# One query token against 256 MB of cached keys and values: which engine sets how many parts of each key unit aside, and where the scratch lies

## The chip, the cores and the metric

The kernel runs on one core of one Trainium2 chip. The metric is the device time of one execution in microseconds (us), the median of several runs. Everything is float32.

## The reference

One token x of 512 elements goes through two branches, and a gate mixes them. Branch a is attention with 32 query heads over 8 key/value heads (four query heads share one) and 32,768 cached positions of 128 elements per key/value head. Branch b is a gated feed-forward block of width 1792.

```
g = sigmoid((x * gate_w).sum(-1))
q = x @ wq                                  # 512 -> 32 heads x 128
scores = q . k_cache * 128 ** -0.5          # 8 kv heads x 32768 positions
o = softmax(scores) . v_cache
a = o @ wo                                  # 4096 -> 512
b = (silu(x @ w1) * (x @ w3)) @ w2          # 512 -> 1792 -> 512
out = g * a + (1 - g) * b
```

k_cache and v_cache have 134 MB each, the weights together some 28 MB. Each byte is used once for one token, so 296 MB must come from HBM.

## The kernel before

**Units.** The keys are cut into 16 units of 8 MB, the values too. Unit t of the keys holds a quarter of the positions of two key/value heads: 128 partitions with 64 KB each, the first 32 KB from the one head (z = 0), the second from the other (z = 1). There are two big buffers, `big_a` and `big_b`, of a unit each (R = 8192 elements is half a unit in one partition). By `where` (L301) key units 0 and 2 go to big_b, all the others to big_a; wq starts in big_a. From the fifth unit on, big_b holds value units.

**A key unit.** Keys lie with the position along the partitions and must be turned. A half unit (z) is cut into four parts c of 32 of the head's 128 elements; a part has 64 x 32 = 2048 elements in each partition. For each part DVE transposes 32 x 32 blocks into `kt0` or `kt1` in turn (L336), and PE multiplies the result with the window of queries, four products (L323). So a unit takes eight transposes, (z, c) from (0, 0) to (1, 3). Of these, the last two, (1, 2) and (1, 3), don't read the big buffer: when the unit has landed, ScalarE copies them into `wo_t` (L311 to L313, `set_aside`), a tile of 16 KB in a partition that will hold a quarter of wo at the end of the kernel. So the big buffer is free after six transposes and ScalarE's copy.

**Order and waits.** The program is written out by `Program.add` (L44), which works out from the keys that each operation reads and writes on which semaphores it waits. Key "A0" is the first half of big_a, "A1" the second, "wo" the tile wo_t. The writing of a buffer waits for its readers. A transpose of keys carries a credit instead of a count (`credit="keys"`, L336): PE takes it in a hardware loop (L679, L684), and whoever must wait for the transpose waits for the PE product that took it (L65 to L66, `via`). PE's instructions inside the loops wait on credits alone (`take`, L665).

**The loop over units** (L465 to L489), for key unit t and, four units behind (LAG = 4), value unit v = t - 4: `set_aside(t)`; the eight parts, with ScalarE's copy of the query window before each half (L317); ScalarE takes the scores out of PSUM (L342); SP issues key unit t + 1 into its buffer; DVE sums up value unit v - 1 (`own`); after every fourth unit the scores are turned by PE (L352) and normalised by DVE and ScalarE (`softmax`, L360 to L389); PE multiplies the value unit v from big_b with its weights (L413); SP issues value unit v + 1 into big_b. After the fourth key unit (t = 3) w1 and w3 are loaded into big_b ahead of key unit 4, multiplied (`hidden_products`, L437), and `hidden` (L452) forms the feed-forward's inner vector on ScalarE and DVE, with row0 as scratch.

**The end** (L576 on): value units 12 to 15 through both big buffers, between them the four quarters of wo into wo_t, which DVE multiplies in (`mix`, L539), and last w2 in five pieces into big_a.

**Queues.** All large loads are issued by SP, one after the other, so an issue that waits holds up those behind it. x, gate_w and the output go by ScalarE's queue. x and gate_w land in `row0` and `row1` (L173, L199), which then hold the queries for a moment (L283 to L286).

Of the kernel before, what the change touches and what calls it, by code (L numbers as in the profile page):

```python
# [116 lines left out]
def kernel(  # L117
# [13 lines left out]
    nc = tc.nc  # L131
    _, HKV, S, DH = k_cache.shape
    D = x.shape[-1]
    F = w1.shape[1]
    HQ = wq.shape[1] // DH
    REP = HQ // HKV
    NC = D // P
# [6 lines left out]
    NB = 64  # L144
    R = NB * DH
    NP = HKV // 2
    NH = 4 * NP
    LAG = 4
    FR = F // P
    FJ = F // 4  # L150
# [4 lines left out]
    pr = Program(nc, tc.alloc_semaphore)  # L155
    pe, dve, act, pool = (
        lambda fn, _e=e, **kw: pr.add(_e, fn, **kw) for e in ("PE", "DVE", "ACT", "POOL")
    )
    V, A, T = nc.vector, nc.scalar, nc.tensor

    def sbuf(name, *shape):
        return nc.alloc_sbuf_tensor(name, [P, *shape], F32)[:]

    big = [sbuf("big_a", 2 * R), sbuf("big_b", 2 * R)]
    wo_t = sbuf("wo_t", 8, D)
    kt = [sbuf(f"kt{i}", NB * 32) for i in range(2)]
    sb = sbuf("sb", 16, 32, 4)
    win = sbuf("win", NP, 4, 48)
# [1 line left out]
    probs = sbuf("probs", 2, 65 * 16)  # L170
    prob = [probs[:, u, :] for u in range(2)]
    pv = sbuf("pv", 33 * 16)
    rows = [sbuf(f"row{i}", 512) for i in range(2)]  # L173
    tmp = sbuf("tmp", 2, 4, P)
    silu = tmp[:, 0].rearrange("p b d -> p (b d)")
    red = [sbuf(f"red{h}", P) for h in range(6)]
    acc = sbuf("acc", 512)
    otp = sbuf("otp", 8, 32)
    htp = sbuf("htp", FR, 32)
# [7 lines left out]
    def load(dst, src, writes, over=()):  # L187
        lanes[0] += 1
        lane = f"load{lanes[0] % 12}"
        return pr.add(  # L190
            "SP", lambda: nc.sync.dma_start(dst, src), writes=writes, over=[*over, lane], inc=lane, by=16, also=lane,  # L191
        )

    def region(b, z):
        return big[b][:, z * R:(z + 1) * R]
# [11 lines left out]
    mt, mtt, mark = sbuf("mt", 32), sbuf("mtt", 32), sbuf("mark", 1)  # L207
# [14 lines left out]
    for src, dst, view, axes in (  # L222
# [9 lines left out]
        s = tiles[src][:, 0:16] if src == "fold" else tiles[src]  # L232
        dve(lambda s=s, d=tiles[dst], v=view, a=axes: V.tensor_reduce(d, s.rearrange(v, **a), axis=AX.X, op=ALU.add),
            reads=[src], writes=[dst])
# [24 lines left out]
    for c in range(NC):  # L259
# [19 lines left out]
        reads=["gate0"], writes=["gate1"])  # L279
# [4 lines left out]
    for b in range(2):  # L284
        qt = kt[b][:, 0:512]
        dve(lambda b=b, qt=qt: V.transpose(qt, rows[b]), reads=[f"row{b}"], writes=[f"kt{b}"])  # L286
        for j in range(4):
            w, u = divmod(4 * b + j, 2)
            src = qt[32 * j:32 * j + 32, :].rearrange("p (q c x) -> p x c q", q=4, c=4)[:, 0]
            for e in range(2):  # L290
                r, o = 2 * u + e, 16 + 8 * e + 4 * u
                dst = win[32 * r:32 * r + 32, w, :, o:o + 4]
# [6 lines left out]
    vd = v_cache.rearrange("a h (e p n) d -> (a h) e p (n d)", e=2, p=P)  # L299

    def where(t):  # L301
        return 1 if t in (0, 2) else 0
# [3 lines left out]
        load(big[b], kd[t // 4, t % 4], ["AB"[b] + str(z) for z in range(2)])  # L306


    spare = wo_t.rearrange("p k e -> p (k e)").rearrange("p (n r) -> p n r", n=NB)

    def set_aside(t):  # L311
        src = region(where(t), 1).rearrange("p (n r) -> p n r", n=NB)[:, :, 64:128]
        act(lambda: A.copy(spare, src), reads=["AB"[where(t)] + "1"], writes=["wo"])  # L313

    def window(t, z):
        return act(
# [4 lines left out]
    def scores_part(c):  # L321
        for g in range(4):
            ins = T.matmul(  # L323
                ps_s[32 * g:32 * g + 32, :], winc[:, c, :], kt[c % 2][:, 512 * g:512 * g + 512],
                start=False, stop=False, skip_group_check=True,
            )
        return ins

    def scores(t, z, win_op):
        kin = region(where(t), z).rearrange("p (n c j) -> p c n j", c=4, j=32)  # L330
        for c in range(4):
            src, key = kin[:, c], "AB"[where(t)] + str(z)
            if (z, c) >= (1, 2):
                src, key = spare[:, :, 32 * (c - 2):32 * (c - 2) + 32], "wo"
            dst = kt[c % 2].rearrange("p (n i) -> p n i", i=32)
            k = dve(lambda d=dst, s=src: V.transpose(d, s), reads=[key], writes=[f"kt{c % 2}"], credit="keys")  # L336
            pe(lambda c=c: scores_part(c), reads=[f"kt{c % 2}", "winc"], writes=["s"], loop=True,
               credits=((win_op, 1), (k, 1)) if c == 0 else ((k, 1),))
# [20 lines left out]
    def softmax(w):  # L359
        banks = [f"f{f}" for f in range(4)]  # L360

        dve(lambda: V.tensor_reduce(mt[:, 0:8], turned.rearrange("p (n q) -> p q n", q=8), axis=AX.X, op=ALU.max),  # L362
            reads=banks, writes=["mt"])
        dve(lambda: V.transpose(mtt, mt), reads=["mt"], writes=["mtt"])
        for k in range(4):
            dve(lambda k=k: V.tensor_reduce(quads[0:32, k:k + 1], mtt[32 * k:32 * k + 32, :], axis=AX.X, op=ALU.max),  # L366
                reads=["mtt"], writes=[("quads", k)])
        dve(lambda: V.tensor_reduce(high[0:32, :], quads[0:32, :], axis=AX.X, op=ALU.max),
            reads=[("quads", k) for k in range(4)], writes=["high"])
        for k in range(4):  # L370
            dve(lambda k=k: V.tensor_copy(wide_t[32 * k:32 * k + 32, :], high[0:32, :].to_broadcast([32, 32])),
                reads=["high"], writes=[("wide_t", k)])
        dve(lambda: V.transpose(top, wide_t), reads=[("wide_t", k) for k in range(4)], writes=["top"])
        dve(lambda: V.tensor_tensor(  # L374
            turned.rearrange("p (n q) -> p n q", q=8), turned.rearrange("p (n q) -> p n q", q=8),
            top[:, 0:8].unsqueeze(1).to_broadcast([P, 256, 8]), op=ALU.subtract,
        ), reads=["top"], writes=banks)

        act(lambda: A.copy(mark, ones[:, 0:1]), reads=["ones"], writes=["mark"])
        for u in range(2):  # L380
            act(lambda u=u: A.activation(  # L381
                prob[u][:, 0:1024].rearrange("p (y n q) -> p n y q", y=16, q=4),
                turned.rearrange("p (n y u q) -> p n y u q", n=16, y=16, u=2)[:, :, :, u],
                AF.Exp, scale=SCALE,
            ), reads=[*banks, "mark"], writes=[("prob", u)])
        dve(lambda: V.tensor_reduce(  # L386
            sums[:, 8 * w:8 * w + 8].rearrange("p (u q) -> p u q", u=2),
            probs[:, :, 0:1024].rearrange("p u (n q) -> p u q n", q=4), axis=AX.X, op=ALU.add,
        ), reads=[("prob", u) for u in range(2)], writes=[("sums", w)])  # L389


    def load_values(s):
        return load_credit(big[1], vd[s // 2, s % 2], ["B0", "B1"])

    def load_credit(dst, src, writes):
        return pr.add("SP", lambda: nc.sync.dma_start(dst, src), writes=writes, credit="values", by=16)

    def weights(s):
        u, e = s // 2 % 2, s % 2
# [32 lines left out]

    def load_hidden():
        for z, t in enumerate((w1, w3)):
            load(region(1, z)[:, 0:NC * F], t.rearrange("(p c) f -> p (c f)", c=NC), [f"B{z}"])

    def hidden_products():  # L437
        for z in range(2):
            def ff(z=z):
                t = region(1, z)  # L440
                for c in range(NC):
                    for j in range(4):
                        o = c * F + FJ * j
                        ins = T.matmul(
                            pm[z][32 * j:32 * j + 32, 0:FJ], xp[:, c, :], t[:, o:o + FJ],
                            start=(c == 0), stop=(c == NC - 1),
                        )
                return ins
            pe(ff, reads=[f"B{z}", "xp"], writes=[f"m{z}"])


    def hidden():  # L452
        act(lambda: A.activation(silu[:, 0:FJ], pm[0][:, 0:FJ], AF.Sigmoid), reads=["m0"], writes=["tmp0"])
        dve(lambda: V.tensor_mul(silu[:, 0:FJ], silu[:, 0:FJ], pm[0][:, 0:FJ]), reads=["m0", "tmp0"], writes=["tmp0"])
        dve(lambda: V.scalar_tensor_tensor(
            rows[0][:, 0:FJ].rearrange("p (k a) -> p k a", k=FR), silu[:, 0:FJ].rearrange("p (a k) -> p k a", k=FR),
            gate[:, 1:2], pm[1][:, 0:FJ].rearrange("p (a k) -> p k a", k=FR), op0=ALU.mult, op1=ALU.mult,
        ), reads=["tmp0", "gate1", "m1"], writes=["row0"])
        dve(lambda: V.transpose(htp.rearrange("p k a -> p (k a)"), rows[0][:, 0:FJ]), reads=["row0"], writes=["htp"])


    load_keys(0)
# [184 lines left out]
    for a, b in parts[2:]:  # L647
        ff_down([(htp[:, k, :], w2t[:, k, :], k == 8, k == FR - 1) for k in range(a, b)], reads=["htp", ("w2", a)])
        if a == 8:
# [4 lines left out]
           reads=["res"], inc="row", by=16)  # L654
# [6 lines left out]
    a, b, c, d = flips  # L661
# [63 lines left out]
```

## Time and profile before

| what | value |
|---|---|
| runs | 702.02, 701.26, 701.96 us; median 701.96 |
| the profiled execution, its own time | 699.78 us |
| its span, first to last instruction | 697.7 us |
| mean granted TensorE clock | 0.795 |
| PE, DVE, ScalarE busy | 374.9, 374.6, 105.5 us |
| read from HBM | 296.23 MB, 425 GB/s over the span |
| transposes of keys (L336) | 128, of 2274 to 2285 ns |
| copies aside (L313) | 16, of 3606 to 3607 ns |

The page gives the busy time of each engine, the span in 40 slices, the DMA queues, the chain of work that ended last, and the costliest groups of instructions by line, each with the idle time of its engine ahead of it and what ended that wait. The timeline gives the start and length of each instruction, SP's issues of transfers among them; the trace has also the start and length of each DMA packet. A packet here is what one partition gets from one transfer, so a unit is 128 packets of 64 KB over 16 DMA engines.

### The profile page before, as it was taken

The numbers are of one execution on the slowest core, as the hardware profiler recorded it, in microseconds if no ns is written. First come the engines' busy times: TensorE is split into PE (matmuls) and PEld (weight loads), VectorE is DVE, ScalarE is ACT, GpSimd is POOL, SyncE is SP. The second block draws the span as 40 slices with busy tenths as digits, with TensorE's granted clock in tenths as the row PEclk, the third lists the DMA queues.
The fourth block names the chain that finished last, engine by engine and source line by source line (L and its number), as shares of the span: only waits on it lengthen the run. The fifth ranks groups of instructions, "written<-read, shape, count | busy, mean of one in ns | idle before, by whom it ended". The sixth has DMA issues, their size and how long they took to land. (4 is left out here: it accounts for less than half of the span.)

```text
span 697.7 us, 5701 instructions
## 1 busy us (share of the span) xinstructions
PE 374.9 (54%) x2400; PEld 87.9 (13%) x2400; DVE 374.6 (54%) x263; ACT 105.5 (15%) x112; POOL 2.6 (0%) x15
## 2 busy tenths in 40 slices
PE   1536555555473736466463636474573726565376
PEld 0100100201010101101010101101010101221012
DVE  1049988591734628591725536790816436744121
ACT  0132221320202121120202121210202021100000
POOL 1000000000000000000000000000000000000000
PEclk9958999879687878978696877778687966777589
DMA  9999999999999999999999999999999999999996
GB/s 410 429 421 421 417 412 419 430 428 425 421 447 436 425 428 428 440 432 428 436 428 421 440 443 429 428 425 436 436 440 432 417 432 421 428 452 429 417 417 287
DMA packets 6644, 296.34 MB, mean 425 GB/s; under 512 B 742, under 2 KB 746, under 8 KB 1132
## 3 DMA queue, kind: packets, MB, share of 16 engines
q1 hardware_dynamic: 6624, 296.23, 98.9%
q8 instruction: 5, 0.08, 0.0%
q14 instruction: 3, 0.02, 0.0%
q10 hardware_dynamic: 12, 0.01, 0.0%
HBM read 296.23 MB, written 0.00 MB: 425 GB/s over the span
## 5 line engine op out<-in xcount | busy, mean ns | idle before, releaser
L323 PE MATMUL ps<-kt,winc 128*32 128x512 f32 x1024 | 182.7, 792 | 238.7 <-PEq L667 238.7
L336 DVE STREAM_TRANSPOSE kt<-big_a 128x2048 f32<-128x2048 f32 x84 | 187.1, 2285 | 182.0 <-DMA big_a<-in_A_k_cache_dram 182.0
L413 PE MATMUL ps<-big_b,pv 128*32 128x512 f32 x768 | 89.3, 619 | 0.0
L313 ACT COPY wo_t<-big_a 128x4096 f32<-128x4096 f32 x14 | 50.5, 3606 | 174.0 <-DMA big_a<-in_A_k_cache_dram 174.0
L323 PEld LDWEIGHTS ps<-kt,winc 128*32 128x32 f32 x1024 | 26.3, 121 | 391.0 <-issue 391.0
L336 DVE STREAM_TRANSPOSE kt<-wo_t 128x2048 f32<-128x2048 f32 x32 | 71.6, 2274 | 0.0
L239 PE MATMUL ps<-acc 128*128 128x512 f32 x34 | 26.3, 866 | 21.8 <-PEq L667 20.3
L342 ACT COPY sb<-ps 128x512 f32<-128x512 f32 x16 | 17.1, 1067 | 135.1 <-PE ps L323 135.1
L541 DVE SCALAR_TENSOR_TENSOR acc<-wo_t,own_rows,acc 128x512 f32<-128x512 f32 x24 | 18.0, 752 | 32.1 <-DMA wo_t<-in_A_wo_dram 31.3
L336 DVE STREAM_TRANSPOSE kt<-big_b 128x2048 f32<-128x2048 f32 x12 | 26.7, 2284 | 11.1 <-DMA big_b<-in_A_k_cache_dram 11.1
L413 PEld LDWEIGHTS ps<-big_b,pv 128*32 128x32 f32 x768 | 23.8, 114 | 65.6 <-issue 65.6
L317 ACT COPY winc<-win 128x128 f32<-128x128 f32 x32 | 9.8, 307 | 109.8 <-PE ps L323 109.7
L554 PE MATMUL ps<-big_b,probs 128*32 128x512 f32 x128 | 18.0, 718 | 13.9 <-DMA big_b<-in_A_v_cache_dram 13.9
L554 PE MATMUL ps<-big_a,probs 128*32 128x512 f32 x128 | 18.5, 742 | 11.3 <-DMA big_a<-in_A_v_cache_dram 11.3
L362 DVE TENSOR_REDUCE mt<-turned 128x8 f32<-128x2048 f32 x4 | 9.2, 2292 | 24.0 <-PE turned L352 24.0
L386 DVE TENSOR_REDUCE sums<-probs 128x8 f32<-128x2048 f32 x4 | 14.9, 3737 | 10.8 <-ACT probs L381 10.8
L265 PE MATMUL turned<-big_a,xp 128*32 128x512 f32 x64 | 9.0, 725 | 11.9 <-DMA big_a<-in_A_wq_dram 11.9
L429 DVE TENSOR_REDUCE red<-tmp 128x128 f32<-128x1024 f32 x6 | 11.6, 1926 | 0.2
L239 PEld LDWEIGHTS ps<-acc 128*128 128x128 f32 x34 | 6.3, 232 | 39.3 <-issue 37.7
L381 ACT ACTIVATE probs<-turned 128x1024 f32<-128x1024 f32 x8 | 7.8, 1021 | 22.4 <-DVE turned L374 22.3
L278 DVE TENSOR_SCALAR gate<-gate 128x1 f32<-128x1 f32 x1 | 0.2, 155 | 20.0 <-ACT gate L277 20.0
L352 PEld LDWEIGHTS turned<-ident,sb 128*128 128x128 f32 x64 | 9.3, 169 | 3.3 <-issue 3.3
(85 smaller groups left out, 123.2 us busy)
## 6 DMA issues: line engine op xcount, KB each, us to landing
wo_t<-in_A_wo_dram SPq DMA_DIRECT2D x4, 2048.0 KB, 18.1
big_b<-in_B_w_dram SPq DMA_DIRECT2D x2, 3584.0 KB, 19.9
big_b<-in_A_v_cache_dram SPq DMA_DIRECT2D x1, 4096.0 KB, 27.4
big_b<-in_A_v_cache_dram SPq DMA_DIRECT2D x2, 2048.0 KB, 34.0
big_a<-in_B_w_dram SPq DMA_DIRECT2D x2, 1024.0 KB, 21.2
big_a<-in_B_w_dram SPq DMA_DIRECT2D x1, 768.0 KB, 23.7
big_a<-in_B_w_dram SPq DMA_DIRECT2D x1, 512.0 KB, 24.4
big_a<-in_B_w_dram SPq DMA_DIRECT2D x1, 256.0 KB, 24.6
```

What stands on the lines that cost most here:

```text
L239: return T.matmul(ps_s, acc[:, 0:P], acc, start=True, stop=False, skip_group_check=True)
L313: act(lambda: A.copy(spare, src), reads=["AB"[where(t)] + "1"], writes=["wo"])
L317: lambda: A.copy(winc, win[:, t // 4, :, 16 - 16 * z:48 - 16 * z]),
L323: ins = T.matmul(ps_s[32 * g:32 * g + 32, :], winc[:, c, :], kt[c % 2][:, 512 * g:512 * g + 512], start=False, stop=False, skip_group_chec ...
L336: k = dve(lambda d=dst, s=src: V.transpose(d, s), reads=[key], writes=[f"kt{c % 2}"], credit="keys")
L342: lambda: A.copy(sb[:, :, :, t % 4], ps_s.rearrange("p (n i) -> p n i", i=32)),
L352: ins = T.transpose(pf[f][:, P * a:P * a + P], sb[:, 4 * f + a].rearrange("p i m -> p (i m)"), ident)
L386: dve(lambda: V.tensor_reduce(sums[:, 8 * w:8 * w + 8].rearrange("p (u q) -> p u q", u=2), probs[:, :, 0:1024].rearrange("p u (n q) -> p u ...
L413: ins = T.matmul(ps_o[32 * t:32 * t + 32, :], pv[:, o:o + 32], big[1][:, n * P:(n + 4) * P], start=((z, g) == (0, 0)), stop=((z, g) == (1, ...
L429: dve(lambda: V.tensor_reduce(red[h], tmp.rearrange("p e b d -> p d (e b)"), axis=AX.X, op=ALU.add), reads=["tmp0", "tmp1"], writes=[("red ...
L541: dve(lambda k=k: V.scalar_tensor_tensor(acc, wo_t[:, k, :], own_rows[:, w, k:k + 1], acc, op0=ALU.mult, op1=ALU.add,), reads=["wo", ("own ...
L554: ins = T.matmul(ps_o[32 * t:32 * t + 32, :], prob[u][:, o:o + 32], vt[:, n * P:(n + 4) * P], start=((e, z, g) == (0, 0, 0)), stop=((e, z, ...
```

## The change

ScalarE sets three parts of each key unit aside in place of two: (1, 1), (1, 2) and (1, 3). The tile for them, `aside`, has 24 KB in a partition; wo_t becomes its first 16 KB. Of key unit 3 (t = LAG - 1) a fourth part, (1, 0), is copied as well, by a second copy, into the last 8 KB of big_b, which is free at that time. So that it stays free, w3 is loaded right behind w1 (from element 7168 of big_b in place of 8192) and the two end at element 14336. The first value unit overwrites that place and waits for the part's reader too (`over=["extra"]`).

The tiles row0 and row1 go: x, gate_w and the queries use the first 1024 elements of `probs` half 0, where the softmax puts its weights later, and the softmax's Exp waits for the readers of row0 and row1. `hidden` uses the second half of `tmp` in place of row0.

```diff
-    wo_t = sbuf("wo_t", 8, D)
+    aside = sbuf("aside", NB * 96)
+    wo_t = aside[:, 0:8 * D].rearrange("p (k e) -> p k e", k=8)
...
-    rows = [sbuf(f"row{i}", 512) for i in range(2)]
+    rows = [probs[:, 0, 512 * i:512 * i + 512] for i in range(2)]
     tmp = sbuf("tmp", 2, 4, P)
-    silu = tmp[:, 0].rearrange("p b d -> p (b d)")
+    silu, prod = (tmp[:, i].rearrange("p b d -> p (b d)") for i in range(2))
...
-    spare = wo_t.rearrange("p k e -> p (k e)").rearrange("p (n r) -> p n r", n=NB)
+    spare = aside.rearrange("p (n r) -> p n r", n=NB)
+    extra = big[1][:, 2 * NC * F:2 * R].rearrange("p (n r) -> p n r", n=NB)

     def set_aside(t):
-        src = region(where(t), 1).rearrange("p (n r) -> p n r", n=NB)[:, :, 64:128]
-        act(lambda: A.copy(spare, src), reads=["AB"[where(t)] + "1"], writes=["wo"])
+        src, key = region(where(t), 1).rearrange("p (n r) -> p n r", n=NB), "AB"[where(t)] + "1"
+        act(lambda: A.copy(spare, src[:, :, 32:128]), reads=[key], writes=["wo"])
+        if t == LAG - 1:
+            act(lambda: A.copy(extra, src[:, :, 0:32]), reads=[key], writes=["extra"], over=["B1"])
...
-            if (z, c) >= (1, 2):
-                src, key = spare[:, :, 32 * (c - 2):32 * (c - 2) + 32], "wo"
+            if (z, c) >= (1, 1):
+                src, key = spare[:, :, 32 * (c - 1):32 * (c - 1) + 32], "wo"
+            elif z == 1 and t == LAG - 1:
+                src, key = extra, "extra"
...
-            ), reads=[*banks, "mark"], writes=[("prob", u)])
+            ), reads=[*banks, "mark"], writes=[("prob", u)], over=["row0", "row1"])
...
-        return load_credit(big[1], vd[s // 2, s % 2], ["B0", "B1"])
-
-    def load_credit(dst, src, writes):
-        return pr.add("SP", lambda: nc.sync.dma_start(dst, src), writes=writes, credit="values", by=16)
+        return pr.add(
+            "SP", lambda: nc.sync.dma_start(big[1], vd[s // 2, s % 2]), writes=["B0", "B1"], over=["extra"],
+            credit="values", by=16,
+        )
...
-            load(region(1, z)[:, 0:NC * F], t.rearrange("(p c) f -> p (c f)", c=NC), [f"B{z}"])
+            load(big[1][:, z * NC * F:(z + 1) * NC * F], t.rearrange("(p c) f -> p (c f)", c=NC), [f"B{z}"])
...
-                t = region(1, z)
+                t = big[1][:, z * NC * F:(z + 1) * NC * F]
...
-            rows[0][:, 0:FJ].rearrange("p (k a) -> p k a", k=FR), silu[:, 0:FJ].rearrange("p (a k) -> p k a", k=FR),
+            prod[:, 0:FJ].rearrange("p (k a) -> p k a", k=FR), silu[:, 0:FJ].rearrange("p (a k) -> p k a", k=FR),
             gate[:, 1:2], pm[1][:, 0:FJ].rearrange("p (a k) -> p k a", k=FR), op0=ALU.mult, op1=ALU.mult,
-        ), reads=["tmp0", "gate1", "m1"], writes=["row0"])
-        dve(lambda: V.transpose(htp.rearrange("p k a -> p (k a)"), rows[0][:, 0:FJ]), reads=["row0"], writes=["htp"])
+        ), reads=["tmp0", "gate1", "m1"], writes=["tmp1"])
+        dve(lambda: V.transpose(htp.rearrange("p k a -> p (k a)"), prod[:, 0:FJ]), reads=["tmp1"], writes=["htp"])
```

## The prediction

> **What bounds the kernel now.** The page's second part first, then its third.
>
> ```profile
> DMA  9999999999999999999999999999999999999996
> GB/s 410 429 421 421 417 412 419 430 428 425 421 447 436 425 428 428 440 432 428 436 428 421 440 443 429 428 425 436 436 440 432 417 432 421 428 452 429 417 417 287
> q1 hardware_dynamic: 6624, 296.23, 98.9%
> ```
>
> DVE and PE are busy 54% of the span, the 16 DMA engines 98.9% of it, all by SP's one queue. So nothing that an engine does matters unless it delays a transfer, and I looked for the time that the queue loses. Next, the groups by shape:
>
> ```profile
> L336 DVE STREAM_TRANSPOSE kt<-big_a 128x2048 f32<-128x2048 f32 x84 | 187.1, 2285 | 182.0 <-DMA big_a<-in_A_k_cache_dram 182.0
> L313 ACT COPY wo_t<-big_a 128x4096 f32<-128x4096 f32 x14 | 50.5, 3606 | 174.0 <-DMA big_a<-in_A_k_cache_dram 174.0
> L317 ACT COPY winc<-win 128x128 f32<-128x128 f32 x32 | 9.8, 307 | 109.8 <-PE ps L323 109.7
> L401 ACT COPY pv<-probs 128x512 f32<-128x512 f32 x12 | 7.5, 621 | 0.0
> ```
>
> Then the landings of the key units: where ScalarE's copy (L313) or DVE's first transpose begins out of a wait for the DMA (the timelines of both):
>
> ```profile
> 102.30 13.28 DVE L336 STREAM_TRANSPOSE kt<-big_a 128x2048 f32<-128x2048 f32 x6 [2.25 <-DMA big_a<-in_A_k_cache_dram]
> 140.54 3.61 ACT L313 COPY wo_t<-big_a 128x4096 f32<-128x4096 f32 x1 [3.05 <-DMA big_a<-in_A_k_cache_dram]
> 179.40 3.61 ACT L313 COPY wo_t<-big_a 128x4096 f32<-128x4096 f32 x1 [17.22 <-DMA big_a<-in_A_k_cache_dram]
> 218.22 3.61 ACT L313 COPY wo_t<-big_a 128x4096 f32<-128x4096 f32 x1 [17.43 <-DMA big_a<-in_A_k_cache_dram]
> 257.66 3.61 ACT L313 COPY wo_t<-big_a 128x4096 f32<-128x4096 f32 x1 [18.67 <-DMA big_a<-in_A_k_cache_dram]
> 296.36 3.61 ACT L313 COPY wo_t<-big_a 128x4096 f32<-128x4096 f32 x1 [5.37 <-DMA big_a<-in_A_k_cache_dram]
> ```
>
> I call the key units K0 to K15, the value units V0 to V15. One key and one value unit lie between most landings, and the quickest such pair takes 38.69 us (K12 at 451.58 to K13 at 490.27). A unit alone takes 19.35 (K0 43.66 to K1 63.01). The trace's record of each DMA packet agrees: a 64 KB packet takes 2.418 us on one engine, each engine has 8 in a unit, 8 x 2.418 = 19.34. w1 and w3 take 16 packets of 1.062 = 16.99. Against that floor the landings lose: K2 0.04, K3 0.57, K4 1.91 (140.54 - 102.30 = 38.24 against 16.99 + 19.34), K5 0.17, K6 0.13, K7 0.75, K9 0.06, K12 0.37, K15 1.05, the others 0.02 or less: 5.13 us from K0 to K15 (568.72). From K15 to wo's third part (660.93) come four units and three parts of wo, 77.38 + 14.69 = 92.07 us by packets, and 92.21 pass: 0.12 or so more. After that the queue is full to the end. In all 5.25 us are lost.
>
> Where, is told by SP's timeline beside the packets:
>
> ```profile
> 78.37 0.33 SPq L191 DMA_DIRECT2D big_a<-in_A_k_cache_dram  x1
> 117.71 0.33 SPq L191 DMA_DIRECT2D big_a<-in_A_k_cache_dram  x1
> 131.56 0.33 SPq L396 DMA_DIRECT2D big_b<-in_A_v_cache_dram  x1
> 156.12 0.33 SPq L191 DMA_DIRECT2D big_a<-in_A_k_cache_dram  x1
> 233.70 0.33 SPq L191 DMA_DIRECT2D big_a<-in_A_k_cache_dram  x1
> ```
>
> A key unit is issued only shortly before the first DMA engine has finished the transfer ahead of it. I call the time between the two the lead: K3 1.98 us (80.35 - 78.37), K4 -0.29 (117.42 - 117.71), K5 1.84, K7 2.17, K12 2.20, K15 2.00, V12 1.97 (it follows K15 into big_a); K2, K6, K8 to K11, K13 and K14 2.4 to 3.1. Value units have 5.9 to 9. Averaged over the 16 engines, waiting and overlong first packets cost 0.1 to 0.9 us where the lead is under 2.5 (1.7 at K4), 0.03 to 0.19 between 2.6 and 3.1, about 0.03 with a value unit. By landings: leads under 2.3 lose 0.12 to 1.91, those of 2.4 to 3.1 lose 0.04 on average, long ones none.
>
> What holds the issue:
>
> ```profile
> SPq L191 <- PE ps L323: 191.4, 18, 14.5
> SPq L110 <- ACT wo_t L313: 178.9, 15, 15.0
> ```
>
> SP waits for ScalarE's copy first and for PE last: a transpose tells SP nothing itself, the scores product (L323) that takes it does. K5: six transposes out of big_a from 141.55, 13.30 us, the product 1.27 later, issue at 156.12.
>
> **The change, part by part.**
> Three parts set aside: five transposes read the unit where six did, so SP is released one transpose earlier, 13.3 / 6 = 2.22 us (2.28 by the group's row). Every lead of K2 to V12 grows by that. The unit is transposed eight times as before, and a transpose from the set-aside tile costs 2274 ns against 2285.
> ScalarE's copy: three rows of copies (128 elements 307 ns, 512 in 621, 4096 in 3606) lie on 0.19 + 0.833 per 1000 elements, so 6144 take 5.31 us, 1.70 more, 16 times. It begins at the landing; the first transpose that reads it is now the sixth, 11.1 us after the landing, and the release comes at 11.1 + 1.3. The cover is 5.8 us. The window copy queued behind it on ScalarE waits for PE's fourth product anyway, about 10 us after the landing. Cost nothing; without that cover it would be 1.7 a unit.
> The fourth unit (K3): another copy of 2048 elements, 1.90 us. Both end 7.2 us after ScalarE starts at 102.38; four transposes and a product end at 102.30 + 8.9 + 1.3 or later. K4's lead grows by two transposes, to 4.2. The new waits (big_b's tail free, V0 after its reader) look back at products finished some 9 us before the copy, and at a transpose finished before K4's landing, while V0 waits for w1's and w3's products as now.
> The scratch: x and gate_w land in a probs half that nothing else uses before 132; the softmax's added wait is for readers done by 35 us. w3 lies right behind w1, same bytes. hidden() writes tmp where it wrote row0, same shapes. Nothing, each bounded by the 0.65 to 0.98 us of such a row, once, on DVE around 140 (below, K5).
>
> **What is late next.** Leads of 4.2 to 5.3 do not occur in the trace. They lie between those of 2.4 to 3.1 (0.04 lost on a landing) and those above 5.9 (0.01): I take 0.03, the ends being 0.01 and 0.13 (K6). K5 is different: DVE works off the softmax and hidden() until 141.64 and only then begins K4. K4 will land 2.5 us earlier (0.04 + 0.57 + 1.91), at 138.0, but DVE comes free only as much earlier as K3 lands, 0.61, at 141.0. K5 goes out at 141.0 + 11.1 + 1.3 = 153.4, and the engines want it at 157.96 - 2.52 = 155.4: a lead of 2.0. There I leave the mean of the landings with leads of 1.8 to 2.2 (0.57, 0.17, 0.75, 0.37, 1.05, 0.12): 0.5, ends 0.1 and 1.05.
> Sum: 5.25 - 0.5 - 14 x 0.03 = **4.3 us** saved, and the last DMA and what follows it (1.5 us from 693.45) move with it. The profiled execution took 699.78 for a span of 697.7; it would be 695.5. The runs shown have 701.96, 2.2 above it, with the same kernel; I take the difference as staying: 697.7.
>
> **A rule that speaks against most of this.** The first packet of K4 begins 1.20 us after its issue (117.71 to 118.91), that of wq 1.23, and K4's last engine starts at 120.42, 2.71 after. The Trainium skill, "DMA: Bandwidth & Descriptors", Specifications, gives about 0.6 us to the first byte for a DMA issued from SP. By it a lead of 1.8 would do and only K4 pay; the trace speaks for a longer time, with overlong packets at leads up to 2.5.
>
> **Rivals.**
> Only the dry queue counts: a lead above the 1.2 us to the first packet is enough, and what K3, K7, K12 and K15 lose is a drift between engines that comes whatever the lead. Then K4's 1.91 goes, or, of it, the 1.24 in which its engines stood empty: 700.1 to 700.7. For it: K9 had overlong packets (0.53 on average) and lost only 0.06 on its landing. Against it: no value unit shows such a loss. 0.13.
> Nothing that can be measured: the early engines' stalls shrink, but the slowest engine of each transfer sets its landing and keeps its pace, so under 0.7 us goes: 701.5. 0.06.
> It doesn't do what it says: SP is still released by the sixth product. Then K4 alone gains little; the same 701.5, and counted with the case before.
> Slower: ScalarE's copy becomes the last to release big_a. It decides from a copy longer than the 14.6 us that the release takes now, and three quarters of a unit would have to cost 4 times the row of half a unit. At 16 us the leads shrink by 1.4, to about 1, and 15 key transfers lose what lies between K15's 1.05 and K4's 1.91, less what they lose now: some 1.2 x 15 = 18 us, 720. Nothing in the rows speaks for it, and the transposes beside the copy are no slower than the others (2285 against 2274 ns). 0.04.
>
> **How the numbers follow.** Forecast 0.77, rivals as above. 697.7 is the likeliest. The low end: the 5.25 whole and 0.4 of spread between runs (701.26 to 702.02), 696.3. The high end takes in the dry-queue case, 700.7. A measurement can tell some 0.2%, 1.4 us, from no change. Faster: the forecast and half of the dry queue, 0.84; within: the other half and the third case, 0.12; slower 0.04.
>
> **What would show it.** ScalarE's copy at 5.3 us in SP's wait, ended by a PE product 12.4 us after the landing; K4 issued near 112.5 with DMA work still queued; the pairs of landings at 38.69 to 38.75 save K4 to K5; no packet group overlong at a key unit's start. Wrong it would be if pairs still lost 0.4 to 1 with leads above 4, if the transposes slowed beside the longer copy, or if a loss moved to the value units.

## The result and the profile after

The changed kernel takes 697.22 us in the median of 9 runs (695.61 to 698.32), the kernel before 701.72 in 9 runs beside it (698.87 to 702.72): a ratio of 0.9936, interval 0.9921 to 0.9951, 4.5 us. The forecast was 697.7 against 701.96, a gain of 4.3. The profiled execution took 695.61 us with a span of 693.5, against 699.78 and 697.7: 4.2 us, where the sum was 4.3.

The page after, first the DMA queue, then the groups of the transposes and of the copies aside:

```profile
q1 hardware_dynamic: 6624, 296.23, 99.1%
L343 DVE STREAM_TRANSPOSE kt<-big_a 128x2048 f32<-128x2048 f32 x69 | 154.1, 2288 | 179.2 <-DMA big_a<-in_A_k_cache_dram 178.3
L316 ACT COPY aside<-big_a 128x6144 f32<-128x6144 f32 x14 | 74.4, 5313 | 169.5 <-DMA big_a<-in_A_k_cache_dram 169.5
L343 DVE STREAM_TRANSPOSE kt<-aside 128x2048 f32<-128x2048 f32 x48 | 106.6, 2271 | 0.0
```

DVE makes as many transposes (69 and 48 in these rows, 11 more out of big_b), no slower; the copy is the 5.31 us of the prediction. ScalarE is busy 134.6 us in place of 105.5, and that shows nowhere in the time. SP's timeline after has the issues of K4, V0, K5, K6 and K7:

```profile
111.91 0.33 SPq L192 DMA_DIRECT2D big_a<-in_A_k_cache_dram  x1
130.95 0.33 SPq L401 DMA_DIRECT2D big_b<-in_A_v_cache_dram  x1
153.34 0.33 SPq L192 DMA_DIRECT2D big_a<-in_A_k_cache_dram  x1
190.24 0.33 SPq L192 DMA_DIRECT2D big_a<-in_A_k_cache_dram  x1
228.70 0.33 SPq L192 DMA_DIRECT2D big_a<-in_A_k_cache_dram  x1
```

K4 is issued 5.8 us earlier than before (117.71), 4.3 us before the first DMA engine has finished w3 (116.18 by the packets). Times of packets are given here as the trace has them, on the same axis as SP's issues. The prediction's stand 0.23 us later: it has the first packet of K4 at 118.91, and the trace has it at 118.68. So all its leads are 0.23 us too long (K3 1.75, K4 -0.52, K5 1.62, K7 1.94, K12 1.97, K15 1.77); their order and its sum don't change by it.

ScalarE's timeline after has the landings of K4 to K8:

```profile
138.22 5.31 ACT L316 COPY aside<-big_a 128x6144 f32<-128x6144 f32 x1 [1.33 <-DMA big_a<-in_A_k_cache_dram]
177.59 5.31 ACT L316 COPY aside<-big_a 128x6144 f32<-128x6144 f32 x1 [15.06 <-DMA big_a<-in_A_k_cache_dram]
216.29 5.31 ACT L316 COPY aside<-big_a 128x6144 f32<-128x6144 f32 x1 [17.97 <-DMA big_a<-in_A_k_cache_dram]
255.00 5.31 ACT L316 COPY aside<-big_a 128x6144 f32<-128x6144 f32 x1 [18.01 <-DMA big_a<-in_A_k_cache_dram]
293.69 5.32 ACT L316 COPY aside<-big_a 128x6144 f32<-128x6144 f32 x1 [5.37 <-DMA big_a<-in_A_k_cache_dram]
```

From 177.59 on the pairs are 38.69 to 38.71 us apart, the floor; K7, which lost 0.75 before, loses nothing, and K15, which lost 1.05, 0.02. K3 lands at 101.76 (before 102.30), K4 36.46 behind it (38.24). The one pair that still loses is K4 to K5, 39.37: 0.68. DVE's timeline shows why:

```profile
135.06 3.75 DVE L393 TENSOR_REDUCE sums<-probs 128x8 f32<-128x2048 f32 x1 [3.34 <-ACT probs L388]
138.73 0.61 DVE L461 TENSOR_TENSOR tmp<-tmp,ps 128x448 f32<-128x448 f32 x1
139.38 0.99 DVE L462 SCALAR_TENSOR_TENSOR tmp<-tmp,gate,ps 128x448 f32<-128x448 f32 x1
140.40 0.65 DVE L466 STREAM_TRANSPOSE htp<-tmp 128x448 f32<-128x448 f32 x1
140.97 11.10 DVE L343 STREAM_TRANSPOSE kt<-big_a 128x2048 f32<-128x2048 f32 x5
```

K4 has landed by 138.22, and DVE is still at the softmax and hidden() until 140.97. So K5 goes out at 153.34 with a lead of 1.53.

### The profile page after: what moved, and what is told of

Same layout as the page of the kernel before. It is cut to its first block, busy times and chain, and to the rows that moved or that the text cites. A ratio compares the mean times of both kernels' runs of the same rounds, so it can differ in the third digit from the quotient of the medians.

```text
span 693.5 us, 5702 instructions
## 1 busy us (share of the span) xinstructions
PE 367.7 (53%) x2400; PEld 86.7 (13%) x2400; DVE 374.4 (54%) x263; ACT 134.6 (19%) x113; POOL 2.6 (0%) x15
## 5 line engine op out<-in xcount | busy, mean ns | idle before, releaser
L328 PE MATMUL ps<-kt,winc 128*32 128x512 f32 x1024 | 177.6, 772 | 238.5 <-PEq L674 238.5
L343 DVE STREAM_TRANSPOSE kt<-big_a 128x2048 f32<-128x2048 f32 x69 | 154.1, 2288 | 179.2 <-DMA big_a<-in_A_k_cache_dram 178.3
L316 ACT COPY aside<-big_a 128x6144 f32<-128x6144 f32 x14 | 74.4, 5313 | 169.5 <-DMA big_a<-in_A_k_cache_dram 169.5
L343 DVE STREAM_TRANSPOSE kt<-aside 128x2048 f32<-128x2048 f32 x48 | 106.6, 2271 | 0.0
L548 DVE SCALAR_TENSOR_TENSOR acc<-aside,own_rows,acc 128x512 f32<-128x512 f32 x24 | 18.0, 752 | 34.6 <-DMA aside<-in_A_wo_dram 33.8
L240 PE MATMUL ps<-acc 128*128 128x512 f32 x34 | 24.1, 799 | 21.8 <-PEq L674 20.3
L343 DVE STREAM_TRANSPOSE kt<-big_b 128x2048 f32<-128x2048 f32 x11 | 24.5, 2282 | 9.6 <-DMA big_b<-in_A_k_cache_dram 9.6
L316 ACT COPY aside<-big_b 128x6144 f32<-128x6144 f32 x2 | 10.6, 5312 | 5.4 <-DMA big_b<-in_A_k_cache_dram 5.4
```

Of the source, the lines that this page charges most:

```text
L240: return T.matmul(ps_s, acc[:, 0:P], acc, start=True, stop=False, skip_group_check=True)
L316: act(lambda: A.copy(spare, src[:, :, 32:128]), reads=[key], writes=["wo"])
L328: ins = T.matmul(ps_s[32 * g:32 * g + 32, :], winc[:, c, :], kt[c % 2][:, 512 * g:512 * g + 512], start=False, stop=False, skip_group_chec ...
L548: dve(lambda k=k: V.scalar_tensor_tensor(acc, wo_t[:, k, :], own_rows[:, w, k:k + 1], acc, op0=ALU.mult, op1=ALU.add,), reads=["wo", ("own ...
```

## The experiments

My theory: what a key unit loses depends on its lead, and the longer leads are the whole gain. The rivals: only the dry queue at K4 counted, or something else in the change brought the gain. The times below are medians; a ratio is to runs of the kernel before on the same chip, whose medians were 701.1 to 701.3.

**The longer lead of K4 alone** (e1): two parts aside for each unit, four for K3.

```diff
+        lo = 1 if t == LAG - 1 else 2
-        act(lambda: A.copy(spare, src[:, :, 32:128]), ...)
+        act(lambda: A.copy(spare[:, :, 32 * (lo - 1):96], src[:, :, 32 * lo:128]), ...)
...
-            if (z, c) >= (1, 1):
+            if (z, c) >= (1, 1 if t == LAG - 1 else 2):
```

> The changed kernel, but with two parts set aside for every key unit except K3, which keeps its four. Only K4 has the longer lead. My theory (every key unit's lead counts): K2, K3 and K6 to V12 lose again what they lost before, about 3 us on the landings, K4 nothing, and K5, which now has neither the old late landing of K4 nor the earlier release, has a lead near 0.4 us and loses 1 to 1.5: in all some 4 us above the changed kernel, 701, about 0.8 under the kernel before. The rival (only a queue that runs dry costs, so K4 was all of the gain): within 1 us of the changed kernel, 697 to 698.

701.06 us, ratio 0.9988 (0.9966 to 1.001). The time is the one expected, but the trace gets there another way. K3 loses 1.8, and from K3 (103.48) to K5 (181.71) pass 78.23 us against a floor of 75.03: K4's gain comes back as a loss of 3.2 at K5, where I had expected 1 to 1.5. K6 to K15, which were to lose again what they lost before, lose 0.5 in all, 0.4 of it at K12. SP's timeline of this kernel, K4, V0, K5:

```profile
113.70 0.33 SPq L192 DMA_DIRECT2D big_a<-in_A_k_cache_dram  x1
134.19 0.33 SPq L402 DMA_DIRECT2D big_b<-in_A_v_cache_dram  x1
159.69 0.33 SPq L192 DMA_DIRECT2D big_a<-in_A_k_cache_dram  x1
```

K5 is issued 3.6 us after the first engine has come free (156.14), where I had expected a lead near 0.4, because K3 had landed late and the chain from K3's last scores through the softmax sets DVE's start, not K4's landing. The engines stand empty for 4.0 us on average. So the queue ran dry in this run too, only one unit later, and its time doesn't decide against the dry-queue rival. That K6 to K15 lose so little fits their leads, 2.5 to 3.5 here against 1.8 to 2.9 before: after the dry queue at K5 the 16 engines start a unit within 0.8 to 1.3 us of each other, before within 1.5 to 2.0, and the lead is counted from the first of them.

**Three parts for all, no fourth** (e2): the second copy and its branch are taken out.

> The changed kernel without the fourth part of K3: three parts of every key unit. My theory: K4's lead is 2.2 us shorter, about 2.0, and its landing loses 0.2 to 1; K5's lead grows by as much as K4 lands later, so it loses less. Together 697.2 to 698.0, 0 to 0.8 above the changed kernel, and no other landing changes. The rival (the dry queue at K4 is all of the gain, and only the fourth part cures it): above 698.6.

697.07 us in 8 runs (695.22 to 700.37), ratio 0.9947 (0.9922 to 0.9973), just under the 697.2 to 698.0 expected. By the medians the fourth part is worth nothing that I can tell; the profiled execution, 698.57 us and so one of the longer ones, loses 2.96 from K3 to K5 (101.58 to 179.57), by the packets most of it at K5. So the third part brings the gain that the medians show; whether the fourth adds some tenths stays open.

**The scratch alone** (e3): the changed layout, two parts aside for every unit.

```diff
-        act(lambda: A.copy(spare, src[:, :, 32:128]), ...)
-        if t == LAG - 1: ...
+        act(lambda: A.copy(spare[:, :, 32:96], src[:, :, 64:128]), ...)
...
-            if (z, c) >= (1, 1):
+            if (z, c) >= (1, 2):
...
-            elif z == 1 and t == LAG - 1: ...
```

> Only the moved scratch and the new places of w3 and of the set-aside tile; two parts set aside of every unit, as before. My theory: it costs and brings nothing, 701.7 as before (within 1 us), K4 landing 38.2 us behind K3 with some 1.9 lost. The rival (other addresses and the freed rows changed something by themselves): nearer to 697 than to 701.7.

701.56 us, ratio 0.9986 (0.9966 to 1.0006): the move costs and brings nothing that can be measured. K4 was worse off in this trace than I expected: it lands 39.54 us behind K3 (103.76 to 143.30), 3.2 lost. K3 itself lost 2.0 with a lead of 1.13, and K7 and K15 nothing, with leads of 2.8 and 2.7.

**Everything changed but the lead** (e4): the sixth transpose is entered as a reader of the big buffer, which it isn't, so SP waits for it as before.

```diff
-            k = dve(lambda ...: V.transpose(d, s), reads=[key], ...)
+            k = dve(lambda ...: V.transpose(d, s), reads=[key, *(["AB"[where(t)] + "1"] if (z, c) == (1, 1) else [])], ...)
```

> The changed kernel in all, but SP's load of the next key unit waits for the product of the sixth transpose as well, as it did before: same copies, same scratch, old leads. The transpose of part (1, 1) is entered as a reader of the big buffer, which it isn't. My theory: the lead is the whole gain, so it falls back to 701.7, within 1 us of the kernel before, with key units issued 1.8 to 3.1 us before the engines come free and pairs that lose up to 1 us. The rival (something else in the change gives the gain, such as DVE reading from another tile): it stays at 697 to 698.

701.51 us, ratio 0.9999 (0.9977 to 1.0021). Same copies, same tiles, same transposes, and the gain is gone. This is the run that carries the explanation: the earlier release of SP is the gain, and the 29 us of added ScalarE work and the moved scratch are none of it. In its trace the losses lie at K3, K4 and K5 (1.7, 1.5 and 0.9, with leads of 1.28, -0.63 and -0.59), not at K7 and K15.

**A still later release** (e5): the same line with (1, 2), so that SP waits for the seventh product.

> The changed kernel, but SP's load of the next key unit waits for the product of the seventh transpose (part (1, 2) entered as a reader of the big buffer). Each lead is 2.2 us shorter than before the change: between -2.5 (K4) and 0.9, most near 0.3. My theory: the first packet comes 1.2 us after the issue, so the engines stand empty about 0.9 us and the first packets are overlong by some 0.5: 1.0 to 1.9 a key unit, as K4 lost at a lead of -0.3. Over 15 units 15 to 25 us above the kernel before less the 5 that it loses there: 712 to 722. The rival (losses are a drift between engines that does not depend on the lead): at most the empty time, 0.9 x 15 = 13 less nothing, and no overlong packets, near 710 or under.

717.99 us, ratio 1.0249 (1.0223 to 1.0276), inside the 712 to 722. First packets take longer than 2.42 us by 0.4 to 0.8 us on the mean of the engines at nearly every key unit, and the engines stand empty for 0.3 to 2.1. One transpose of release is worth 4 us in the one direction and 16 in the other.

**The copy made twice** (e6).

```diff
-        act(lambda: A.copy(spare, src[:, :, 32:128]), reads=[key], writes=["wo"])
+        for _ in range(2):
+            act(lambda: A.copy(spare, src[:, :, 32:128]), reads=[key], writes=["wo"])
```

> The changed kernel with each copy aside made twice, one behind the other. My theory: 10.6 us of copies end before the sixth transpose, which is 11.1 us after the landing, so the cover of 5.8 us just holds and the time is that of the changed kernel, within 1 us; K4, with 12.5 us of copies against 10 of transposes, loses some of its lead but keeps over 1.5. The rival (ScalarE's copy is on the path, so each us of it counts): 5.3 us a unit over 16 units, some 40 us or more slower.

701.30 us, ratio 1.0004 (0.9989 to 1.0019): 4 us of the gain gone, where I had expected none. ScalarE's timeline of this kernel at K2 and K3:

```profile
84.10 1.08 ACT L350 COPY sb<-ps 128x512 f32<-128x512 f32 x1 [8.06 <-PE ps L329]
85.17 10.66 ACT L317 COPY aside<-big_b 128x6144 f32<-128x6144 f32 x2
95.74 0.29 ACT L323 COPY winc<-win 128x128 f32<-128x128 f32 x1
106.03 10.66 ACT L317 COPY aside<-big_a 128x6144 f32<-128x6144 f32 x2
116.59 1.89 ACT L319 COPY big_b<-big_a 128x2048 f32<-128x2048 f32 x1
```

and DVE's:

```profile
82.87 11.30 DVE L344 STREAM_TRANSPOSE kt<-big_b 128x2048 f32<-128x2048 f32 x5
95.93 6.88 DVE L344 STREAM_TRANSPOSE kt<-aside 128x2048 f32<-128x2048 f32 x3 [1.76 <-ACT aside L317]
102.74 4.52 DVE L344 STREAM_TRANSPOSE kt<-big_a 128x2048 f32<-128x2048 f32 x2
118.59 2.31 DVE L344 STREAM_TRANSPOSE kt<-big_b 128x2048 f32<-128x2048 f32 x1 [4.01 <-ACT big_b L319]
```

Among the first units, 19.35 us apart, ScalarE must first take the scores of the unit before out of PSUM. It starts its copy 2.3 us (K2) and 3.3 us (K3) after DVE has begun the unit. So of the 5.8 us that one copy leaves, 3.5 and 2.5 are left there, less than a second copy of 5.3, and K3 has the fourth part besides. DVE waits, K4 is issued at 118.56 and K5 at 163.20, and the DMA engines stand empty at K4, V0 and K5 for 2.2, 2.2 and 2.5 us on average. Later most pairs are at 38.7. Two causes were possible: the first units alone, or a doubled copy anywhere.

**The copy made twice from K4 on** (f1): `range(2 if t >= LAG else 1)`.

> The changed kernel with each copy aside made twice from K4 on, once for K0 to K3. With the copies doubled everywhere, K5 and the landings behind it lost nothing in the trace, and all that was lost lay at K3, K4, V0 and K5, where units come every 19.35 us and ScalarE starts 1.6 to 3.3 us after the landing. My theory: in the steady part the cover of 5.8 us holds, so the time is that of the changed kernel, 696 to 698, and no pair after K5 loses more than 0.2. The rival (the doubled copy costs a little everywhere): near 701 again.

697.20 us, ratio 0.9943 (0.992 to 0.9965), that of the changed kernel. So the first units it is; in the steady part the cover holds with twice the copy.

**The copy made three times** (e7): `range(3)`.

> The same with each copy made three times, 15.9 us. The cover is gone: the window of the second half, queued behind the copies on ScalarE, comes 16.2 us after the landing, so PE's fifth product comes about 17.4 after it and SP is released some 5 us later than in the changed kernel. My theory: leads near -0.5, about 1.9 lost on most key units, 27 us, and among the first four units, where a unit comes every 19.35 us, each unit takes some 25 us of copies, transposes and products, 15 us more: 730 to 745. The rival of the prediction that was priced at 18 us (copy the last to release): 715 to 725. If the copy mattered in no way: 697.

743.70 us, ratio 1.0603 (1.0578 to 1.0628), inside the 730 to 745. The window copy queued behind the copies holds up PE's fifth product, as expected. In the prediction this case was priced at 18 us over the kernel before; it costs 42 (743.70 - 701.25).

**hidden() one unit later** (e8): the only short lead that is left is K5's, and DVE's 2.3 us of hidden() ahead of K4 can wait.

```diff
-        if t == LAG - 1:
+        if t == LAG:
             hidden()
```

> The changed kernel with the feed-forward's inner vector formed one unit later, behind the transposes of K4 instead of ahead of them. My theory: K5's lead of 2.3 us is the last short one and loses 0.68 on its landing; DVE is free 2.3 us earlier for K4, and K5 is issued that much earlier, lead above 4: 0.5 to 0.7 us faster than the changed kernel, 696.6, and the pair K4 to K5 takes 38.7 instead of 39.37. The rival (K5's loss comes from something else about that place, such as the packets of w1 and w3 being of another size): the pair keeps 39.2 to 39.5 and the time stays at 697.2.

694.83 us (694.69 to 694.94 in 5 runs), ratio 0.9905 (0.9882 to 0.9928). This version beats both kernels. ScalarE's timeline at K4 and K5, then SP's issue of K5:

```profile
137.72 5.31 ACT L316 COPY aside<-big_a 128x6144 f32<-128x6144 f32 x1 [3.15 <-DMA big_a<-in_A_k_cache_dram]
176.43 5.31 ACT L316 COPY aside<-big_a 128x6144 f32<-128x6144 f32 x1 [14.71 <-DMA big_a<-in_A_k_cache_dram]
```

```profile
151.06 0.33 SPq L192 DMA_DIRECT2D big_a<-in_A_k_cache_dram  x1
```

K5 is issued 2.3 us earlier than in the changed kernel and lands 38.71 behind K4: its loss is gone. The profiled executions differ by the 0.7 expected (694.94 and 695.61). But the medians differ by 2.4 us, not 0.6, and the spread shrank from 2.7 us to 0.25. Either the chips differ or the changed kernel's profile was one of its best runs. Both again, on one chip:

**The changed kernel again** (f2) and **hidden() later again** (f3).

> The changed kernel once more, beside the next one on one chip. Its runs spread over 2.7 us (695.61 to 698.32) and those of the kernel with hidden() one unit later over 0.25. My theory: the profiled run was one of the quickest, and K5, issued at a lead near 2 us, loses between 0.5 and 3 from run to run, depending on when TensorE's granted clock is 0.5 among K2 to K4 and holds up DVE. So 696.5 to 698 as a median, with K5's landing losing more than the 0.67 of the first profile where the run is slower than 695.6. The rival (the spread is the chip's own): spread 0.3 to 1 on this chip, like the other's, or K5's loss the same 0.67 in a slower run.

> The changed kernel with hidden() one unit later, again, on the same chip as the kernel ahead of it. Theory: 694.6 to 695.2 with a spread under 0.6, no key unit's landing losing anything but K12's, and 2 to 3 us under the changed kernel. The rival: the difference of 2.4 us was between chips, and here it is the 0.67 of the trace.

696.92 us (695.94 to 699.20, 12 runs) and 694.90 (694.68 to 695.32, 6 runs), ratios 0.9942 (0.9923 to 0.9962) and 0.9906 (0.9874 to 0.9939). So the 2 us belong to the kernels, not to the chips. The timeline of the changed kernel's second profile (696.53 us) at four places: PE ahead of K3's first product, DVE at K3 and at K4, SP at K5:

```profile
103.45 2.05 PE L240 MATMUL ps<-acc 128*128 128x512 f32 x2 [1.28 <-PEq L674]
...
107.28 4.50 DVE L343 STREAM_TRANSPOSE kt<-big_a 128x2048 f32<-128x2048 f32 x2 [1.27 <-PE ps L328]
...
142.21 11.11 DVE L343 STREAM_TRANSPOSE kt<-big_a 128x2048 f32<-128x2048 f32 x5
...
154.58 0.33 SPq L192 DMA_DIRECT2D big_a<-in_A_k_cache_dram  x1
```

The granted clock there (PEclk in the windows 101 to 103 and 103 to 106) was 0.50; in the first profile it was 1.00 at that place and the same product took 1.10. PE ends K2 later, ScalarE takes the scores out later, DVE waits 1.27 us for a free kt tile, and the whole chain to K5's issue is 1.24 us later (154.58 against 153.34). From K3 to K5 this run loses 1.01, the first 0.80. That is only 0.2 of the 0.9 us between the two executions. The rest lies behind V15's last piece, which comes 20.54 us behind wo's third part (677.43 - 656.89) in the one and 19.53 in the other; see the last section. That longer losses of the same kind make up the other runs, up to 699.2, was not seen in a trace of the changed kernel, but in that of f1, which is the same kernel up to K4. PE turns the scores of K0 to K3 there at a granted clock of 0.72 (window 120 to 126), in the first profile at 1.00; first that profile's row, then f1's with DVE's start on K4 and SP's issue of K5:

```profile
122.83 1.91 PE L359 MATMUL turned<-ident,sb 128*128 128x128 f32 x16
...
123.20 3.01 PE L360 MATMUL turned<-ident,sb 128*128 128x128 f32 x16
142.50 11.10 DVE L344 STREAM_TRANSPOSE kt<-big_a 128x2048 f32<-128x2048 f32 x5
154.87 0.33 SPq L192 DMA_DIRECT2D big_a<-in_A_k_cache_dram  x1
```

DVE is 1.5 us later than in the first profile, so is K5's issue, and from K3 to K5 f1 loses 2.2. How much of the spread comes from the clock stays open; that most of it goes when K5 is issued earlier is shown by e8 and f3.

**The kernel before with hidden() later** (f4): the same edit, nothing else.

> The kernel before the change, with hidden() one unit later and nothing else. Theory: only K5's lead grows, by about 1 us up to where K4's late landing sets DVE's start; K2 to K4 and K6 to V12 keep their short leads and lose what they lost. 700 to 701.3, 0.2 to 1.5 under the kernel before. The rival (DVE's work ahead of K4 was the cause of most of the losses): below 698.

700.51 us, ratio 0.9988 (0.996 to 1.0017). Alone, the reorder gives nothing that can be measured. In its trace K5's lead grows from 1.62 to 2.84 and its loss goes from 0.17 to 0.02, and K4 still loses 1.9. That it pays more in the changed kernel fits the trace there, where K5's is the only short lead left.

## Why the prediction was right, point by point

- **The bound.** Transfers, and only what delays them: shown by e4 (all the added work, no gain, no loss) and e5 (no more work than e4, 16 us lost).
- **The release one transpose earlier.** K7 is issued 12.41 us after K6's landing (228.70 - 216.29), predicted 12.4. K4 at 111.91 against "near 112.5", K5 at 153.34 against 153.4.
- **Where the loss lay.** The sum was read from one execution, and that its size held is in part luck: 1.8 of its 5.25 us lay at K7 and K15, where the traces of e1, e3, e4 and f4, with the old release for these units, lose nothing. From K0 to K15 the first three lose 4.8 to 5.9 us all the same, most of it from K3 to K5; f4 loses 2.8. Nor does a short lead fix the loss: with 1.7 to 1.8 us, K5 in e3 and K15 in f4 lost 0.01, and K15 before lost 1.05. How much the short leads from K6 on cost as a rule stays open.
- **Copies and scratch at nothing.** Right in the changed kernel (e3 for the scratch). The cover of 5.8 us behind the copy was counted from the landing. That holds from K4 on (f1); among K1 to K3 ScalarE starts late, by 0.6 to 1.7 us in the changed kernel's trace and up to 3.3 in e6, and the cover is that much smaller. It did not run out in the changed kernel, so the sum was not touched.
- **What is late next.** K5, as foretold: lead 1.53 against 2.0 (1.8 on the trace's axis), loss 0.68 against 0.5. Its size moves with TensorE's clock among the first units (f1, f2), which the prediction did not see.
- **From the trace to the median.** The prediction took the 2.2 us between its profiled execution and the median as staying, without a cause. After the change it is 1.6, in f2 0.4, with hidden() later -0.1 and 0.2: it depends on the kernel and on which execution was profiled. That the median came out within 0.5 us of 697.7 is in part luck.
- **The other landings.** 0.03 each was taken; the trace has 0.13 at K4, 0.13 at K12 and 0.02 or less at the rest, together some 0.35 against the 0.42 of the sum. K12's 0.37 before was put down to a short lead, and that is doubtful (last section). The gap in the leads that the prediction filled by estimate was not quite empty: V8 had 4.94 before (5.17 by its times) and lost nothing.
- **The rivals.** The dry-queue case said that a lead above the time to the first packet is enough. It falls with the traces: K3 lost 2.0 and 1.7 at leads of 1.13 and 1.28 (e3, e4), K5 lost 0.68 at 1.53 after the change, and 4.2 us went where K4 had 1.91 to give. The times of e1 and e4 don't decide, since the queue ran dry in both. Its drift, which comes whatever the lead, is not excluded for what K7 and K15 lost before. The slower case would have had its price wrong: 18 us against 42 with three copies, because I put only the release behind the copy and not the window for PE, nor the first units.
- **The first packet.** Behind a dry queue it began 0.95 to 1.03 us after the start of the issue (not 1.20), some 0.63 after its end. The Trainium skill, "DMA: Bandwidth & Descriptors", Specifications, gives about 0.6 us to the first byte; counted from the end of the issue the trace agrees with it, so the prediction's "longer time" was its 0.23 and the length of the issue. What doesn't follow is that a longer lead is enough: K5 lost 0.68 with 1.53. The last of the 16 engines began K4 2.48 us after the issue before the change.

## What to carry to other kernels

When one DMA queue is busy 99% of the span, compare the distance between landings with bytes by packet time: what is above that floor is all that can be won, and the distance between an issue and the end of the transfer ahead of it says where it is. Here transfers of 8 MB wanted their issue some 2.5 us or more ahead; a shorter lead cost up to 2 us, and a queue that ran dry more (3.2 in e1 and in e3). Work added to an idle engine to release a buffer earlier is free only up to its start, so look at what that engine does when the data lands; and a wait with no slack shows as spread between runs: 2.7 to 3.3 us with K5's late issue, 0.25 to 0.6 without it.

## What the runs showed of the hardware that was not expected

**Instructions travel with the data.** K12 loses between nothing and 0.64 us, whatever its lead. ScalarE's timelines at K11 and K12, first of e8, then of f4, where the leads differ by a transpose:

```profile
408.63 5.31 ACT L316 COPY aside<-big_a 128x6144 f32<-128x6144 f32 x1 [17.53 <-DMA big_a<-in_A_k_cache_dram]
447.97 5.31 ACT L316 COPY aside<-big_a 128x6144 f32<-128x6144 f32 x1 [7.29 <-DMA big_a<-in_A_k_cache_dram]
```

```profile
410.93 3.61 ACT L313 COPY wo_t<-big_a 128x4096 f32<-128x4096 f32 x1 [18.00 <-DMA big_a<-in_A_k_cache_dram]
450.20 3.61 ACT L313 COPY wo_t<-big_a 128x4096 f32<-128x4096 f32 x1 [5.47 <-DMA big_a<-in_A_k_cache_dram]
```

39.34 and 39.27 us against 38.70. In the traces looked at for it (the kernel before, the changed one, e3, e4, e8) a packet of 8 KB of the queue q14, which the page of the profile calls "instruction", runs between 427.8 and 432.9 us for some 0.32 us, and right behind it one data packet takes 3.07 to 3.08 us in place of 2.42. The landing is late where the engine that had it was near the last: in e8 it was 0.30 us ahead of the last one, and K12 lost 0.64; in f1 it was 2.25 ahead, and K12 lost 0.01. The five packets of 16 KB of q8 take 0.88 to 1.07 us each; the one at 675.22 in the second profile of the changed kernel fits the 1.0 us by which V15's last piece was late there, but the first profile has one at 674.93 and no such delay. No run took these packets away, so that they are the cause is argued from their place and size.
